# Moving six query transposes and their copy behind the last value product of batch 0, in a one-core attention and feed-forward kernel

## The chip, the cores and the metric

The kernel runs on one core of a Trainium2 chip. The core has five engines with queues of their own: TensorE (PE in the profile, PEld for its weight loads), VectorE (DVE), ScalarE (ACT), GpSimd (POOL) and SyncE (SP, which here only issues DMAs). The metric is the device time of one execution in microseconds (us); less is better.

## The reference

Attention over 4 batches and 8 heads of 768 positions with head size 64. Heads 0, 2 and 6 are causal over all positions ("retrieval"); the five others see four sink positions and a window of 64. The outputs of the eight heads stand side by side as 512 features of 3072 tokens and go through a two-layer network with a PReLU between the layers.

```python
mask = np.where(retr[0, :, 0, 0, None, None], full_mask, stream_mask)
scores = np.where(mask[None, :, :, :], scores, -1000000000.0)
a = np.exp(scores - np.max(scores, axis=-1, keepdims=True))
a = a / (np.sum(a, axis=-1, keepdims=True) + 1e-09)
attn_out = np.matmul(a, v)
x = attn_out.transpose(0, 2, 1, 3).reshape(B * S, H * D)
h = x @ w_in                                  # 512 -> 2048
g = np.maximum(h, 0.0) + alpha * np.minimum(h, 0.0)
out = g @ w_out                               # 2048 -> 512
```

## The kernel before, in words

Everything is a named item, and the list `ORDER` at the head of the file says in which order the items are put into the program (the loop at line 809). There is no scheduler behind it: each engine runs its own instructions in the order in which `ORDER` names them, and waits by semaphores for what it needs from the others. So moving a name in the list moves its instructions in the queue of each engine on which it has any, and nowhere else.

Attention works on pairs of heads. Number n = 4 * batch + pair, with the pairs (2,6), (1,5), (0,4), (3,7). So n = 3 is the last pair of batch 0 (heads 3 and 7, both windowed), and n = 5 is the second pair of batch 1 (heads 1 and 5). The items that matter here, with the engine that runs them:

- `Lq5`, `Cq5`: load of the queries of n = 5 (SP) and their cast to bf16 (`cast_q`, line 317; POOL for n = 5 and n = 4).
- `Tq5`: `to_array`, line 365, six 128x128 transposes on TensorE of the cast queries into one PSUM bank. `tq5`: `put_q`, line 370, one copy of that bank by ScalarE into the transposed queries qT. `Tk4` and `tk4.0`, `Tq4` and `tq4` are the same for other keys and queries.
- `S3.1.0`, `S3.1.1`: scores of n = 3, second head (TensorE, matmuls of line 415, each with a mask matmul of line 503). `s3.1.0`, `s3.1.1`: their exponentials (ScalarE, line 525). `S3.1.0` fills two banks and is the last score item of batch 0.
- `A3.0`, `A3.1`: the value product of each head of n = 3, 13 matmuls with the exponentials as weights (`AV`, line 554). `a3.0`, `a3.1`: division by the row sums (VectorE, lines 564 and 565).
- `X3`, `x3`: seven transposes of the result of n = 3 (TensorE, line 579) and the copy into xT (VectorE, line 584).
- `P0.2.0` and the like: matmuls of the first layer (`P1`, line 599) for token block 0 and feature block 2. In the first blocks they are split by head pair, part 0 being the pairs n = 0 and 1 (two matmuls), part 1 n = 2 (one), part 2 n = 3 (one). `p...` (line 604, ScalarE) and `g...` (line 611, VectorE) do the PReLU and free the bank. `O...` (line 619) is the second layer.

The batches overlap: the head of batch 1 (loads, casts, transposes) lies between the end of the attention of batch 0 and its feed-forward work. PSUM has eight banks. `take` gives an item the bank among its choices that was freed longest ago in the order of the list, and `give` records the freeing; so which bank an item gets is fixed by the order alone, when the program is built.

The part of the order around the change, before it:

```
... s3.1.1 S3.1.0 x1 P0.0.0 x2 P0.0.1 A3.0 P0.1.0 P0.1.1 Tq5 tq5 Lk6 Lq4 Lq6 Ck4.1 kfz3 nr
Cv3.1 s3.1.0 A3.1 Lv7 Lv5 Lq7 Ck5.0 wi3 a3.0 P0.2.0 P0.3.0 P0.3.1 a3.1 X3 x3 ns kfz1 P0.2.1
Tk4 near2 P1.2 ...
```

Of the kernel before, what the change touches and what calls it, by code (L numbers as in the profile page):

```python
# [25 lines left out]
g0.11 m8.0.2 tk5.1 wo2 Lv6 Lv4 P0.10 P0.8 p0.8 Tk7 g1.10 wo3 Cq4 Lk9 P0.12 P1.8 p0.10 g0.8 p0.12 g0.10 Tq4 P0.6 P0.9
p0.3 Ck6.1 g0.3 tq4 P0.4.0 P0.5.0 Tk6 P0.4.1 p1.8 g1.8 tk7.0 p0.9 g0.9 Cq6 P0.5.1 P0.5.2 p0.5 g0.12 p0.6 tk6.1 P0.4.2
g0.6 g0.5 tk6.0 S4.0.5 P0.7 p0.7 P1.6 g0.7 P1.4 s4.0.5 p0.4 Tq6 m4.1.2 tk7.1 g0.4 Cv5 p1.6 g1.6 O0.1.0 tq6 S4.0.3
O0.2.0 O0.2.1 S5.1.1 S5.0.0 S4.0.1 S6.1.0 m14.0.2 p1.4 g1.4 s5.0.0 O0.1.1 s4.0.3 s4.0.1 O0.2.2 S5.0.2 S5.1.0 S4.0.2
S5.1.2 s6.1.0 m4.0.1 Cv7 O0.3.0 s5.0.2 s5.1.2 s5.1.1 s4.0.2 O0.1.2 s5.1.0 O0.1.3 o0.1 Cq7 Cv4 O0.3.1 m5.1.0 m8.1.2  # L30
m5.0.2 m4.0.3 m5.1.2 S4.0.0 S4.1.4 S5.0.1 S4.0.4 S4.1.0 s4.0.4 s5.0.1 Lk10 m5.0.1 O0.2.3 O0.3.2 Tq7 m5.0.0 o0.2 s4.1.0
m4.0.4 m5.1.1 A5.1 s4.0.0 m4.0.0 a5.1 O0.3.3 tq7 S7.0.0 S7.0.1 S4.1.3 S7.1.1 S6.0.5 S4.1.1 m4.0.5 s4.1.4 o0.3 Lq9
s4.1.3 Ck8 m4.1.3 A5.0 a5.0 X5 s4.1.1 A4.0 s7.0.0 s7.1.1 Lk11 Lq8 s7.0.1 a4.0 s6.0.5 near1 m7.0.0 m7.1.1 m4.1.0 O1.1.0
S7.1.0 S6.0.4 S7.0.2 S4.1.5 S6.0.1 S7.1.2 S6.1.1 O1.1.1 Cv6 s7.1.0 O1.0.0 s4.1.5 m7.0.1 s6.1.1 m4.1.5 m6.1.1 s7.1.2
m6.1.0 s7.0.2 m7.0.2 S6.0.2 S4.1.2 S6.1.2 S6.0.0 s6.0.4 s4.1.2 s6.0.1 s6.1.2 O1.0.1 m6.0.5 m7.1.0 m4.1.1 m4.1.4 m7.1.2
m6.1.2 S6.0.3 A4.1 s6.0.0 m6.0.0 m6.0.1 A7.1 O1.1.2 A6.1 s6.0.3 m6.0.4 m6.0.3 s6.0.2 a4.1 a6.1 A6.0 A7.0 a6.0 O1.1.3
O0.0.0 O0.0.1 O0.0.2 O1.0.2 m10.0.2 O1.0.3 O0.0.3 o0.0 X4 X6 a7.1 a7.0 X7 P2.9 P2.3 p2.9 P3.4 Ck9 Cq9 g2.9 P2.14 p2.14
g2.14 Cq8 p3.4 Lq10 Lq11 Dk8.0 P2.10 p2.10 Dk9.1 o1.0 p2.3 g2.3 g3.4 Dk8.1 P3.2 P3.14 P3.12 P2.8 Dq8 P2.1 P3.8 o1.1
p3.2 Dk9.0 Lv10 g2.10 Dq9 p3.14 P2.7 Ck10 g3.2 p3.12 g3.12 g3.14 P2.2 p2.2 g2.2 Cq10 Dq10 P2.11 p2.1 g2.1 p2.11 p2.8
g2.11 P3.6 P2.5 p2.5 g2.5 P2.13 p2.13 g2.8 g2.13 P2.0 p2.0 g2.0 p2.7 P3.0 p3.0 P2.4 S8.0.5 Lv8 Lv11 P2.15 P2.12 s8.0.5  # L40
Cq11 g3.0 p2.15 g2.7 g2.15 S8.0.0 p2.12 g2.12 Ck11 p3.6 S9.0.2 P2.6 p2.6 g3.6 s8.0.0 p2.4 g2.4 g2.6 s9.0.2 p3.8 P3.10
g3.8 p3.10 O3.0.0 O2.0.0 S8.1.5 s8.1.5 O3.0.1 O2.0.1 g3.10 m8.0.0 Cv8 S8.1.3 S9.0.0 S8.0.3 S9.1.1 S8.0.1 S9.1.0 s8.1.3
s9.1.0 s8.0.1 s9.0.0 s8.0.3 m8.0.3 m8.0.1 O2.0.2 O2.0.3 o2.0 Dk10.1 Lv9 m9.0.0 Cv9 m8.0.5 Dk11.0 m9.1.0 m9.0.2 S8.0.4
S9.0.1 S10.1.1 S8.1.4 Dq11 s8.1.4 Lq13 Lk13 O3.0.2 Dk10.0 s9.1.1 s10.1.1 s9.0.1 s8.0.4 O3.0.3 o3.0 Dk11.1 S10.1.0
S10.1.2 m9.0.1 S11.0.2 S9.1.2 S8.0.2 S11.0.0 s9.1.2 Cv10 m9.1.1 A9.0 s11.0.2 s10.1.0 O2.3.0 m9.1.2 A9.1 a9.0 a9.1 X9
s10.1.2 s11.0.0 O2.3.1 Lq15 Lv14 Lq12 S8.1.0 S11.0.1 S10.0.3 m10.1.0 s8.0.2 S10.0.1 S8.1.2 S8.1.1 S10.0.0 O2.3.2
s8.1.2 s8.1.0 m8.1.4 Cq13 s11.0.1 s8.1.1 m11.0.2 m10.1.2 m8.0.4 m11.0.0 A8.0 s10.0.0 m8.1.5 m10.1.1 O2.3.3 a8.0
S11.1.2 S10.0.4 S11.1.0 S10.0.5 S10.0.2 m8.1.3 m11.0.1 s10.0.3 s10.0.1 S11.1.1 s11.1.2 A10.1 s11.1.1 O2.2.0 O2.1.0
s10.0.4 m6.0.2 m10.0.1 Cv11 m8.1.1 m8.1.0 a10.1 m10.0.4 Ck13 m10.0.0 m11.1.2 A11.0 A8.1 O2.1.1 s10.0.2 s10.0.5 o2.3
s11.1.0 Dk13.0 m11.1.1 m10.0.3 m10.0.5 m11.1.0 A10.0 a11.0 a8.1 a10.0 O3.1.0 A11.1 Cq12 O2.2.1 O2.2.2 O2.2.3 a11.1 X8  # L50
O2.1.2 O3.1.1 O3.1.2 X10 o2.2 O3.1.3 O2.1.3 X11 P4.11 o2.1 P4.14 P5.14 p5.14 P4.4 P4.6 Lk12 P5.0 g5.14 Ck12 p4.4 p4.6
p4.11 P4.13 g4.6 p4.14 g4.11 Lq14 g4.14 P5.12 P4.5 P4.12 p4.13 Dq12 o3.1 p5.0 g4.13 Cq14 g5.0 Dk13.1 p4.5 g4.5 g4.4
Cv14 P4.9 p4.9 g4.9 P4.2 P5.2 Dq13 p5.12 g5.12 P4.10 p5.2 P4.8 P4.1 p4.12 g4.12 g5.2 p4.10 g4.10 Lv15 Dk12.0 Dk12.1
Lv12 p4.1 Lk14 Lv13 Lk15 g4.1 P4.7 P4.0 p4.2 g4.2 p4.8 g4.8 p4.0 p4.7 g4.7 P4.15 Cv12 S13.0.1 s13.0.1 S12.0.5 S12.0.3
P4.3 P5.4 g4.0 s12.0.3 p4.3 s12.0.5 S12.1.5 S12.0.1 S12.0.0 S13.1.1 s13.1.1 Dq14 g4.3 Cq15 Ck14 m12.0.3 O4.3.0 s12.1.5
s12.0.1 O4.3.1 O4.3.2 s12.0.0 p4.15 g4.15 P5.6 P5.10 S12.1.1 S12.0.4 S12.0.2 p5.4 S13.1.0 g5.4 p5.6 s12.0.4 Dk14.0
P5.8 s13.1.0 s12.0.2 p5.8 s12.1.1 m12.0.0 g5.6 O4.3.3 Ck15 p5.10 g5.8 m12.0.1 g5.10 m12.0.4 O5.1.0 Cv13 O5.1.1 O5.1.2
o4.3 Dk14.1 S14.1.1 S14.0.0 S12.1.4 S14.0.1 S14.1.0 S13.0.2 m12.1.1 s14.1.0 s13.0.2 O4.2.0 m12.0.5 A12.0 s14.0.1
s12.1.4 O5.1.3 Dk15.1 s14.1.1 Dk15.0 s14.0.0 a12.0 m14.0.1 Dq15 o5.1 O4.2.1 S13.1.2 S12.1.2 S14.1.2 S14.0.4 m13.1.0
m14.0.0 m13.0.1 S14.0.5 S13.0.0 O4.2.2 O4.2.3 s13.1.2 m13.1.2 m13.1.1 s13.0.0 s14.0.4 s14.0.5 m13.0.2 S12.1.0 m12.1.5  # L60
s14.1.2 S12.1.3 S15.0.0 S14.0.3 m13.0.0 A13.1 o4.2 s12.1.0 s12.1.2 A13.0 s15.0.0 O5.0.0 s12.1.3 s14.0.3 m14.0.4 Cv15
a13.1 O5.0.1 a13.0 S15.0.1 S15.0.2 m12.1.0 S15.1.0 S15.1.2 S15.1.1 S14.0.2 O4.1.0 s15.0.2 s15.1.0 m12.1.4 s14.0.2
s15.1.1 m14.1.1 m14.0.5 m14.1.2 m12.1.3 m14.1.0 A12.1 m14.0.3 A14.1 A14.0 a14.0 s15.1.2 a14.1 m15.0.2 s15.0.1 a12.1
O4.1.1 X13 O4.0.0 O4.0.1 O4.0.2 O4.0.3 m15.0.0 m15.1.1 O4.1.2 m15.0.1 m15.1.2 m15.1.0 A15.0 o4.0 A15.1 a15.0 O4.1.3
a15.1 O5.0.2 X15 O5.0.3 X14 x15 o4.1 o5.0 X12 P6.11 p6.11 P6.2 P6.15 P6.10 p6.10 P7.4 P6.0 P6.1 g6.11 g6.10 p6.1 P6.6
P7.8 p6.15 g6.15 g6.1 p6.0 g6.0 P6.5 p7.4 p6.5 p6.6 g7.4 g6.6 g6.5 P6.3 P6.12 P7.2 p6.3 p6.12 g6.12 p6.2 g6.2 P6.4
p7.8 P7.6 P6.14 g6.3 g7.8 p7.6 p6.4 g7.6 g6.4 P7.10 P6.7 P6.8 p6.8 p6.7 P7.0 P6.9 P6.13 g6.7 p7.2 g7.2 g6.8 p7.10
g7.10 p6.9 P7.14 O6.3.0 P7.12 p6.13 g6.13 p7.12 O6.0.0 O6.0.1 O6.1.0 p7.0 g7.0 g6.9 O6.3.1 O7.0.0 O6.3.2 O6.1.1 p7.14
p6.14 g6.14 g7.12 O6.3.3 o6.3 O6.0.2 O6.1.2 O6.1.3 o6.1 O6.0.3 o6.0 O6.2.0 O6.2.1 O6.2.2 O7.0.1 O7.0.2 O6.2.3 o6.2
m12.0.2 g7.14 L2 l2 O7.0.3 o7.0 L0 L1 l1 warm1 l0  # L70
""".split()


# [776 lines left out]
```

## Time and profile before

| What | Value |
|---|---|
| Time, median of 3 runs | 231.12 us (231.07 to 232.63) |
| Time of the profiled execution | 231.47 us |
| Its span, first to last instruction | 229.8 us |
| Between the two, outside the span | 1.67 us |
| Mean granted TensorE clock | 1.000 |

Where the time goes by stretches of the span; PE, ACT and DVE are busy us:

| Stretch (us) | PE | ACT | DVE | DMA share | What runs |
|---|---|---|---|---|---|
| 27 to 29 | 2.00 | 0.00 | 1.19 | 1.22 | end of the attention of batch 0 |
| 29 to 31 | 0.40 | 1.51 | 0.26 | 1.18 | transposes of n = 5, their copy, exponential of n = 3 |
| 31 to 33 | 2.00 | 0.00 | 0.83 | 1.20 | last value product, first layer begins |
| 33 to 50 | 17.00 | 14.93 | 14.09 | 1.19 | first layer of batch 0, transposes of batch 1 |
| 50 to 57.2 | 6.89 | 6.81 | 4.59 | 1.10 | scores of batch 1 begin |
| 57.2 to 229.8 | 169.49 | 98.07 | 107.93 | 0.70 | the rest |

The trace gives, for each instruction, its start and duration on its engine, and for the idle time before it the engine or DMA whose signal ended it. A matmul's duration contains its way through the array, so that matmuls following one another overlap in the record: four of 512 columns take about 0.86 us, though each is shown with some 0.38. The DMA share is that of 16 DMA engines; values over 1 are overlapping packets.

### The profile page before, as it was taken

How to read it: one execution, taken by the hardware profiler on the slowest of the kernel's cores; microseconds unless marked ns; L12 is line 12 of the kernel's file. 1: busy time of each engine (PE TensorE's matmuls, PEld its weight loads, DVE VectorE, ACT ScalarE, POOL GpSimd, SP SyncE). 2: the span in 40 equal slices, each digit the busy share in tenths (PEclk: the TensorE clock that was granted, in tenths of full speed). 3: DMA queues.
4: the chain of work that ended last, by engine and by line, in shares of the span. 5: the costliest groups of instructions: out<-in, count | busy, mean ns of one | idle time of the engine just before them, and what ended most of it. 6: DMA issues, size and time to landing. Idle time of an engine off the chain costs nothing.

```text
span 229.8 us, 5247 instructions
## 1 busy us (share of the span) xinstructions
PE 221.8 (97%) x2005; PEld 135.1 (59%) x2005; DVE 148.9 (65%) x394; ACT 140.6 (61%) x285; POOL 45.9 (20%) x91
## 2 busy tenths in 40 slices
...
PEclk9999999999999999999999999999999999999999
...
GB/s 190 294 214 219 274 214 277 207 196 227 207 259 146 137 186 216 209 134 187 247 172 234 156 276 178 199 176 93 144 93 38 115 94 0 0 4 0 91 72 113
DMA packets 94957, 37.26 MB, mean 162 GB/s; under 512 B 81980, under 2 KB 93140, under 8 KB 94932
## 3 DMA queue, kind: packets, MB, share of 16 engines
...
q10 hardware_dynamic: 464, 0.40, 0.5%
q8 instruction: 15, 0.25, 0.4%
...
## 4 chain that ended last, share of the span: by engine, by line
PE 88%; ACT 3%; DMA 2%; issue 2%; SPq 1%; POOL 1%; DVE 0%; POOLq 0%; DVEq 0%; ACTq 0%
PE P L599 35%; PE P L619 34%; PE P L554 7%; PE P L432 4%; DMA kf<-in_k_dram 2%; PE P L365 2%; PE P L415 2%; PE P L638 2%; ACT neg L604 1%; PE P L503 1%; SPq L223 1%; PE P L579 1%; PE P L425 1%; ACT kT L394 1%; ACT eS L525 1%
## 5 line engine op out<-in xcount | busy, mean ns | idle before, releaser
L611 DVE SCALAR_TENSOR_TENSOR g<-neg,oma,P 128x256 bf16<-128x256 f32 (+1 forms) x128 | 71.1, 610 | 36.0 <-ACT neg L604 35.5
L599 PE MATMUL P<-xT,w_in_b 128*128 128x512 bf16 (+1 forms) x512 | 86.3, 326 | 0.0
L619 PE MATMUL P<-w_out_b,g 128*128 128x512 bf16 x368 | 85.4, 379 | 0.0
L604 ACT ACTIVATE neg<-P 128x512 f32<-128x512 f32 x96 | 54.1, 600 | 29.0 <-PE P L599 24.6
L599 PEld LDWEIGHTS <-w_in_b 128*128 128x128 bf16 x512 | 49.5, 98 | 31.9 <-DVE g L611 0.2
L619 PEld LDWEIGHTS <-g 128*128 128x128 bf16 x368 | 33.7, 98 | 37.3 <-issue 1.2
L471 ACT ACTIVATE eR<-P 128x448 bf16<-128x448 f32 (+4 forms) x63 | 37.2, 639 | 6.1 <-PE P L432 2.5
L625 ACT COPY ot<-P 128x512 f32<-128x512 f32 x23 | 13.9, 604 | 37.3 <-PE P L619 32.4
L629 POOL DMA_DIRECT2D out_dram<-ot x18 | 10.3, 571 | 115.0 <-ACT ot L625 114.8
L519 ACT ACTIVATE eS<-P 128x352 bf16<-128x352 f32 x45 | 21.0, 497 | 3.7 <-PE P L432 3.7
L565 DVE TENSOR_TENSOR xn<-P,rcp 128x448 bf16<-128x448 f32 (+1 forms) x32 | 19.5, 608 | 1.1
L530 DVE TENSOR_TENSOR eS<-eS,ms_near 128x352 bf16<-128x352 bf16 x45 | 14.5, 338 | 5.0 <-ACT eS L519 4.9
L481 DVE TENSOR_TENSOR eR<-eR,mr_near 128x128 bf16<-128x128 bf16 (+5 forms) x54 | 10.8, 228 | 4.4 <-ACT eR L471 4.4
L554 PE MATMUL P<-vb,eS 128*128 128x65 bf16 x260 | 10.8, 193 | 1.6 <-ACT eS L525 1.6
L564 DVE RECIPROCAL rcp<-P 128x7 f32<-128x7 f32 (+1 forms) x32 | 6.3, 198 | 9.2 <-PE P L554 9.0
L432 PE MATMUL P<-qT,kT 64*128 64x176 bf16 (+13 forms) x181 | 11.7, 251 | 0.3 <-DVE g L611 0.3
L554 PEld LDWEIGHTS <-eS 128*128 128x128 bf16 x260 | 9.5, 97 | 3.9 <-ACT eS L525 1.8
L432 PEld LDWEIGHTS <-kT 64*128 64x128 bf16 x181 | 7.2, 94 | 7.6 <-issue 6.4
L415 PE MATMUL P<-qT,kT 128*128 128x192 bf16 (+14 forms) x68 | 11.3, 251 | 0.3 <-ACT eS L525 0.3
L554 PE MATMUL P<-vb,eR 128*128 128x65 bf16 x276 | 10.1, 193 | 0.0
L554 PEld LDWEIGHTS <-eR 128*128 128x128 bf16 x276 | 9.4, 97 | 1.2
L647 DVE COPY ot<-P 128x128 f32<-128x128 f32 x1 | 0.3, 292 | 14.3 <-PE P L638 14.3
...
## 6 DMA issues: line engine op xcount, KB each, us to landing
...
```

The costliest lines, as they stand in the source:

```text
L415: nc.tensor.matmul(to, keys, queries, start=True, stop=stop)
L432: nc.tensor.matmul(to, keys[own], queries[own], start=True, stop=True)
L471: nc.scalar.activation(ebuf[n, hh][:, lo:hi].rearrange("p (x c) -> p x c", x=len(parts)), P[:, got[0]:got[0] + len(parts), 0:(hi - lo) // ...
L519: nc.scalar.activation(slots, sc[:, 0:352].rearrange("p (s c) -> p s c", c=176), AF.Exp, scale=scale)
L530: nc.vector.tensor_tensor(slots, slots, ms_near[:, 0:2, :] if m == 0 else ms_near[:, 1:3, :], op=ALU.mult)
L554: nc.tensor.matmul(pav[:, i, :], e[:, o:o + 128], vv[:, j, hh, 0:D + 1], start=(m == 0), stop=(m == len(terms) - 1))
L565: nc.vector.tensor_tensor(xn[n][:, 0:nt, D * hh:D * hh + D], pav[:, :, 0:D], rcp.to_broadcast([128, nt, D]), op=ALU.mult)
L599: nc.tensor.matmul(psg[:, w * i:w * (i + 1)], w_in_b[:, c, 128 * fb:128 * (fb + 1)], xT[:, c, o:o + w], start=(x == 0), stop=(x == 3))
L604: nc.scalar.activation(neg[t, f], bank(held["P", t, f][0]), AF.Relu, scale=-1.0)
L611: nc.vector.scalar_tensor_tensor(g_buf[t % 2][:, fb, 0:w], neg[t, f][:, c], oma[:, fb:fb + 1], bank(got[0])[:, c], op0=ALU.mult, op1=ALU.add)
L619: nc.tensor.matmul(bank(held["O", t, s][0]), g_buf[t % 2][:, f, 128 * s:128 * (s + 1)], w_out_b[:, f, :], start=(f == 0), stop=(f == 15))
L625: nc.scalar.copy(ot, bank(got[0]))
```

## The change

`Tq5` and `tq5` move down the list, from before `Lk6` to behind `P0.2.0`. Nothing else is moved.

```diff
-Ck4.0 s3.1.1 S3.1.0 x1 P0.0.0 x2 P0.0.1 A3.0 P0.1.0 P0.1.1 Tq5 tq5 Lk6 Lq4 Lq6 Ck4.1 kfz3 nr Cv3.1 s3.1.0 A3.1 Lv7 Lv5
-Lq7 Ck5.0 wi3 a3.0 P0.2.0 P0.3.0 P0.3.1 a3.1 X3 x3 ns kfz1 P0.2.1 Tk4 near2 P1.2 P0.1.2 P0.2.2 P0.0.2 p1.2 p0.1 g0.1
+Ck4.0 s3.1.1 S3.1.0 x1 P0.0.0 x2 P0.0.1 A3.0 P0.1.0 P0.1.1 Lk6 Lq4 Lq6 Ck4.1 kfz3 nr Cv3.1 s3.1.0 A3.1 Lv7 Lv5 Lq7
+Ck5.0 wi3 a3.0 P0.2.0 Tq5 tq5 P0.3.0 P0.3.1 a3.1 X3 x3 ns kfz1 P0.2.1 Tk4 near2 P1.2 P0.1.2 P0.2.2 P0.0.2 p1.2 p0.1
...
```

The remaining lines of the diff are the same list wrapped differently. On each engine this comes to:

- TensorE: the six transposes of `Tq5` now stand behind the 13 matmuls of `A3.1` and the two of `P0.2.0`, before the three of `P0.3.0` and `P0.3.1`.
- ScalarE: the copy `tq5` and the exponential `s3.1.0` change places.
- VectorE, POOL and SP: the same instructions in the same order.

The banks follow the order. `Tq5` gets bank 1 in place of 0, `P0.2.0` bank 0 in place of 1, `P0.3.0` bank 2 in place of 0 (freed by `s3.1.0`, no longer by `tq5`), `Tk4` bank 3 in place of 2, and `P1.2` bank 1 in place of 3 (freed by `tq5`, no longer by `s3.1.0`). From there on the four banks 0 to 3 are renamed among themselves to the end of the program, and each item's bank is freed by the same item as before. So the first matmul of `P1.2` has a new wait, for `tq5` on ScalarE.

More of the change, by code (lines that the diff above doesn't have):

```diff
@@ L21 @@
 A1.1 a2.0 tq3 s2.1.0 a1.1 S3.0.0 s2.1.1 s3.0.0 A2.1 a2.1 S3.1.1 X1 S3.0.1 s3.0.1 Lk5 wi4 kfz2 Cv3.0 Cq5 Lk7 wi2 X2
-Ck4.0 s3.1.1 S3.1.0 x1 P0.0.0 x2 P0.0.1 A3.0 P0.1.0 P0.1.1 Tq5 tq5 Lk6 Lq4 Lq6 Ck4.1 kfz3 nr Cv3.1 s3.1.0 A3.1 Lv7 Lv5
-Lq7 Ck5.0 wi3 a3.0 P0.2.0 P0.3.0 P0.3.1 a3.1 X3 x3 ns kfz1 P0.2.1 Tk4 near2 P1.2 P0.1.2 P0.2.2 P0.0.2 p1.2 p0.1 g0.1
-Ck5.1 P1.0 P0.3.2 g1.2 P0.15 tk4.0 p0.2 g0.2 p0.15 wo0 p1.0 Lk8 near0 g0.15 g1.0 ro1 P1.12 P1.14 m12.1.2 p0.0 g0.0 wo1
-tk4.1 p1.12 P0.14 g1.12 p0.14 g0.14 P0.13 p0.13 g0.13 P0.11 p1.14 Tk5 Ck7.1 g1.14 P1.10 tk5.0 p0.11 p1.10 Ck6.0 Ck7.0
@@ L26 @@
[L26 to L70, printed above, removed]
+Ck4.0 s3.1.1 S3.1.0 x1 P0.0.0 x2 P0.0.1 A3.0 P0.1.0 P0.1.1 Lk6 Lq4 Lq6 Ck4.1 kfz3 nr Cv3.1 s3.1.0 A3.1 Lv7 Lv5 Lq7
@@ new lines @@
+Ck5.0 wi3 a3.0 P0.2.0 Tq5 tq5 P0.3.0 P0.3.1 a3.1 X3 x3 ns kfz1 P0.2.1 Tk4 near2 P1.2 P0.1.2 P0.2.2 P0.0.2 p1.2 p0.1
+g0.1 Ck5.1 P1.0 P0.3.2 g1.2 P0.15 tk4.0 p0.2 g0.2 p0.15 wo0 p1.0 Lk8 near0 g0.15 g1.0 ro1 P1.12 P1.14 m12.1.2 p0.0
+g0.0 wo1 tk4.1 p1.12 P0.14 g1.12 p0.14 g0.14 P0.13 p0.13 g0.13 P0.11 p1.14 Tk5 Ck7.1 g1.14 P1.10 tk5.0 p0.11 p1.10
+Ck6.0 Ck7.0 g0.11 m8.0.2 tk5.1 wo2 Lv6 Lv4 P0.10 P0.8 p0.8 Tk7 g1.10 wo3 Cq4 Lk9 P0.12 P1.8 p0.10 g0.8 p0.12 g0.10 Tq4
+P0.6 P0.9 p0.3 Ck6.1 g0.3 tq4 P0.4.0 P0.5.0 Tk6 P0.4.1 p1.8 g1.8 tk7.0 p0.9 g0.9 Cq6 P0.5.1 P0.5.2 p0.5 g0.12 p0.6
@@ new lines @@
+tk6.1 P0.4.2 g0.6 g0.5 tk6.0 S4.0.5 P0.7 p0.7 P1.6 g0.7 P1.4 s4.0.5 p0.4 Tq6 m4.1.2 tk7.1 g0.4 Cv5 p1.6 g1.6 O0.1.0
+tq6 S4.0.3 O0.2.0 O0.2.1 S5.1.1 S5.0.0 S4.0.1 S6.1.0 m14.0.2 p1.4 g1.4 s5.0.0 O0.1.1 s4.0.3 s4.0.1 O0.2.2 S5.0.2
+S5.1.0 S4.0.2 S5.1.2 s6.1.0 m4.0.1 Cv7 O0.3.0 s5.0.2 s5.1.2 s5.1.1 s4.0.2 O0.1.2 s5.1.0 O0.1.3 o0.1 Cq7 Cv4 O0.3.1
+m5.1.0 m8.1.2 m5.0.2 m4.0.3 m5.1.2 S4.0.0 S4.1.4 S5.0.1 S4.0.4 S4.1.0 s4.0.4 s5.0.1 Lk10 m5.0.1 O0.2.3 O0.3.2 Tq7
+m5.0.0 o0.2 s4.1.0 m4.0.4 m5.1.1 A5.1 s4.0.0 m4.0.0 a5.1 O0.3.3 tq7 S7.0.0 S7.0.1 S4.1.3 S7.1.1 S6.0.5 S4.1.1 m4.0.5
@@ new lines @@
+s4.1.4 o0.3 Lq9 s4.1.3 Ck8 m4.1.3 A5.0 a5.0 X5 s4.1.1 A4.0 s7.0.0 s7.1.1 Lk11 Lq8 s7.0.1 a4.0 s6.0.5 near1 m7.0.0
+m7.1.1 m4.1.0 O1.1.0 S7.1.0 S6.0.4 S7.0.2 S4.1.5 S6.0.1 S7.1.2 S6.1.1 O1.1.1 Cv6 s7.1.0 O1.0.0 s4.1.5 m7.0.1 s6.1.1
+m4.1.5 m6.1.1 s7.1.2 m6.1.0 s7.0.2 m7.0.2 S6.0.2 S4.1.2 S6.1.2 S6.0.0 s6.0.4 s4.1.2 s6.0.1 s6.1.2 O1.0.1 m6.0.5 m7.1.0
+m4.1.1 m4.1.4 m7.1.2 m6.1.2 S6.0.3 A4.1 s6.0.0 m6.0.0 m6.0.1 A7.1 O1.1.2 A6.1 s6.0.3 m6.0.4 m6.0.3 s6.0.2 a4.1 a6.1
+A6.0 A7.0 a6.0 O1.1.3 O0.0.0 O0.0.1 O0.0.2 O1.0.2 m10.0.2 O1.0.3 O0.0.3 o0.0 X4 X6 a7.1 a7.0 X7 P2.9 P2.3 p2.9 P3.4
@@ new lines @@
+Ck9 Cq9 g2.9 P2.14 p2.14 g2.14 Cq8 p3.4 Lq10 Lq11 Dk8.0 P2.10 p2.10 Dk9.1 o1.0 p2.3 g2.3 g3.4 Dk8.1 P3.2 P3.14 P3.12
+P2.8 Dq8 P2.1 P3.8 o1.1 p3.2 Dk9.0 Lv10 g2.10 Dq9 p3.14 P2.7 Ck10 g3.2 p3.12 g3.12 g3.14 P2.2 p2.2 g2.2 Cq10 Dq10
+P2.11 p2.1 g2.1 p2.11 p2.8 g2.11 P3.6 P2.5 p2.5 g2.5 P2.13 p2.13 g2.8 g2.13 P2.0 p2.0 g2.0 p2.7 P3.0 p3.0 P2.4 S8.0.5
+Lv8 Lv11 P2.15 P2.12 s8.0.5 Cq11 g3.0 p2.15 g2.7 g2.15 S8.0.0 p2.12 g2.12 Ck11 p3.6 S9.0.2 P2.6 p2.6 g3.6 s8.0.0 p2.4
+g2.4 g2.6 s9.0.2 p3.8 P3.10 g3.8 p3.10 O3.0.0 O2.0.0 S8.1.5 s8.1.5 O3.0.1 O2.0.1 g3.10 m8.0.0 Cv8 S8.1.3 S9.0.0 S8.0.3
@@ new lines @@
+S9.1.1 S8.0.1 S9.1.0 s8.1.3 s9.1.0 s8.0.1 s9.0.0 s8.0.3 m8.0.3 m8.0.1 O2.0.2 O2.0.3 o2.0 Dk10.1 Lv9 m9.0.0 Cv9 m8.0.5
+Dk11.0 m9.1.0 m9.0.2 S8.0.4 S9.0.1 S10.1.1 S8.1.4 Dq11 s8.1.4 Lq13 Lk13 O3.0.2 Dk10.0 s9.1.1 s10.1.1 s9.0.1 s8.0.4
+O3.0.3 o3.0 Dk11.1 S10.1.0 S10.1.2 m9.0.1 S11.0.2 S9.1.2 S8.0.2 S11.0.0 s9.1.2 Cv10 m9.1.1 A9.0 s11.0.2 s10.1.0 O2.3.0
+m9.1.2 A9.1 a9.0 a9.1 X9 s10.1.2 s11.0.0 O2.3.1 Lq15 Lv14 Lq12 S8.1.0 S11.0.1 S10.0.3 m10.1.0 s8.0.2 S10.0.1 S8.1.2
+S8.1.1 S10.0.0 O2.3.2 s8.1.2 s8.1.0 m8.1.4 Cq13 s11.0.1 s8.1.1 m11.0.2 m10.1.2 m8.0.4 m11.0.0 A8.0 s10.0.0 m8.1.5
@@ new lines @@
+m10.1.1 O2.3.3 a8.0 S11.1.2 S10.0.4 S11.1.0 S10.0.5 S10.0.2 m8.1.3 m11.0.1 s10.0.3 s10.0.1 S11.1.1 s11.1.2 A10.1
+s11.1.1 O2.2.0 O2.1.0 s10.0.4 m6.0.2 m10.0.1 Cv11 m8.1.1 m8.1.0 a10.1 m10.0.4 Ck13 m10.0.0 m11.1.2 A11.0 A8.1 O2.1.1
+s10.0.2 s10.0.5 o2.3 s11.1.0 Dk13.0 m11.1.1 m10.0.3 m10.0.5 m11.1.0 A10.0 a11.0 a8.1 a10.0 O3.1.0 A11.1 Cq12 O2.2.1
+O2.2.2 O2.2.3 a11.1 X8 O2.1.2 O3.1.1 O3.1.2 X10 o2.2 O3.1.3 O2.1.3 X11 P4.11 o2.1 P4.14 P5.14 p5.14 P4.4 P4.6 Lk12
+P5.0 g5.14 Ck12 p4.4 p4.6 p4.11 P4.13 g4.6 p4.14 g4.11 Lq14 g4.14 P5.12 P4.5 P4.12 p4.13 Dq12 o3.1 p5.0 g4.13 Cq14
@@ new lines @@
+g5.0 Dk13.1 p4.5 g4.5 g4.4 Cv14 P4.9 p4.9 g4.9 P4.2 P5.2 Dq13 p5.12 g5.12 P4.10 p5.2 P4.8 P4.1 p4.12 g4.12 g5.2 p4.10
+g4.10 Lv15 Dk12.0 Dk12.1 Lv12 p4.1 Lk14 Lv13 Lk15 g4.1 P4.7 P4.0 p4.2 g4.2 p4.8 g4.8 p4.0 p4.7 g4.7 P4.15 Cv12 S13.0.1
+s13.0.1 S12.0.5 S12.0.3 P4.3 P5.4 g4.0 s12.0.3 p4.3 s12.0.5 S12.1.5 S12.0.1 S12.0.0 S13.1.1 s13.1.1 Dq14 g4.3 Cq15
+Ck14 m12.0.3 O4.3.0 s12.1.5 s12.0.1 O4.3.1 O4.3.2 s12.0.0 p4.15 g4.15 P5.6 P5.10 S12.1.1 S12.0.4 S12.0.2 p5.4 S13.1.0
+g5.4 p5.6 s12.0.4 Dk14.0 P5.8 s13.1.0 s12.0.2 p5.8 s12.1.1 m12.0.0 g5.6 O4.3.3 Ck15 p5.10 g5.8 m12.0.1 g5.10 m12.0.4
@@ new lines @@
+O5.1.0 Cv13 O5.1.1 O5.1.2 o4.3 Dk14.1 S14.1.1 S14.0.0 S12.1.4 S14.0.1 S14.1.0 S13.0.2 m12.1.1 s14.1.0 s13.0.2 O4.2.0
+m12.0.5 A12.0 s14.0.1 s12.1.4 O5.1.3 Dk15.1 s14.1.1 Dk15.0 s14.0.0 a12.0 m14.0.1 Dq15 o5.1 O4.2.1 S13.1.2 S12.1.2
+S14.1.2 S14.0.4 m13.1.0 m14.0.0 m13.0.1 S14.0.5 S13.0.0 O4.2.2 O4.2.3 s13.1.2 m13.1.2 m13.1.1 s13.0.0 s14.0.4 s14.0.5
+m13.0.2 S12.1.0 m12.1.5 s14.1.2 S12.1.3 S15.0.0 S14.0.3 m13.0.0 A13.1 o4.2 s12.1.0 s12.1.2 A13.0 s15.0.0 O5.0.0
+s12.1.3 s14.0.3 m14.0.4 Cv15 a13.1 O5.0.1 a13.0 S15.0.1 S15.0.2 m12.1.0 S15.1.0 S15.1.2 S15.1.1 S14.0.2 O4.1.0 s15.0.2
@@ new lines @@
+s15.1.0 m12.1.4 s14.0.2 s15.1.1 m14.1.1 m14.0.5 m14.1.2 m12.1.3 m14.1.0 A12.1 m14.0.3 A14.1 A14.0 a14.0 s15.1.2 a14.1
+m15.0.2 s15.0.1 a12.1 O4.1.1 X13 O4.0.0 O4.0.1 O4.0.2 O4.0.3 m15.0.0 m15.1.1 O4.1.2 m15.0.1 m15.1.2 m15.1.0 A15.0 o4.0
+A15.1 a15.0 O4.1.3 a15.1 O5.0.2 X15 O5.0.3 X14 x15 o4.1 o5.0 X12 P6.11 p6.11 P6.2 P6.15 P6.10 p6.10 P7.4 P6.0 P6.1
+g6.11 g6.10 p6.1 P6.6 P7.8 p6.15 g6.15 g6.1 p6.0 g6.0 P6.5 p7.4 p6.5 p6.6 g7.4 g6.6 g6.5 P6.3 P6.12 P7.2 p6.3 p6.12
+g6.12 p6.2 g6.2 P6.4 p7.8 P7.6 P6.14 g6.3 g7.8 p7.6 p6.4 g7.6 g6.4 P7.10 P6.7 P6.8 p6.8 p6.7 P7.0 P6.9 P6.13 g6.7 p7.2
```

3 lines of the change are left out of this document (added).

## The prediction

> **What bounds the kernel now.** I read the page first: how full is TensorE, and who carries the chain that ended last.
>
> ```profile
> PE 221.8 (97%) x2005; PEld 135.1 (59%) x2005; DVE 148.9 (65%) x394; ACT 140.6 (61%) x285; POOL 45.9 (20%) x91
> PEclk9999999999999999999999999999999999999999
> PE 88%; ACT 3%; DMA 2%; issue 2%; SPq 1%; POOL 1%; DVE 0%; POOLq 0%; DVEq 0%; ACTq 0%
> ```
>
> TensorE is busy 97% of the span and is 88% of the chain. A change that moves no work off it can only gain where TensorE stands still, so I looked for its gaps: the chain of waits in order of time, from 28 us on.
>
> ```profile
> 28.35 0.65 PE P L599 x3
> 29.00 0.35 PE P L365 x6
> 29.35 0.02 issue
> 29.37 0.80 ACT qT L370
> 30.17 0.72 ACT eS L525
> 30.89 0.05 issue
> 30.94 0.57 PE P L554 x13
> 31.51 1.08 PE P L599 x5
> ```
>
> The chain leaves TensorE for 1.6 us: `Tq5` (L365), then `tq5` on ScalarE (L370), then the exponential `s3.1.0` (L525), and only then `A3.1` (L554). The timelines of TensorE and of ScalarE say why; columns are start, duration, engine, line and, in brackets, the idle time before it and what ended it.
>
> ```profile
> 27.07 0.25 PE L503 MATMUL P<-nms,ident 128*128 128x192 bf16 x1
> 28.84 0.50 PE L365 MATMUL P<-ident,natq 128*128 128x128 bf16 x6
> 30.94 0.57 PE L554 MATMUL P<-vb,eS 128*128 128x65 bf16 x13 [1.60 <-ACT eS L525]
> 33.42 0.27 PE L599 MATMUL P<-xT,w_in_b 128*128 128x256 bf16 x1
> ```
>
> ```profile
> 29.37 0.80 ACT L370 COPY qT<-P 128x768 bf16<-128x768 bf16 x1 [2.55 <-PE P L365]
> 30.07 0.82 ACT L525 ACTIVATE eS<-P 128x768 bf16<-128x768 f32 x1
> 34.49 1.08 ACT L604 ACTIVATE neg<-P 128x512 f32<-128x512 f32 x2 [3.61 <-PE P L599]
> ```
>
> The last mask matmul of `S3.1.0` ends at 27.07 + 0.25 = 27.32. ScalarE was idle then, and idle until 29.37, because the copy that waits for `Tq5` stands ahead of the exponential in its queue. The exponential was ready 2.7 us before it ran.
>
> **The change part by part.** *ScalarE:* the exponential no longer stands behind the copy. It needs `S3.1.0` (27.32) and runs 0.82: done by about 28.2. *TensorE:* `A3.1` follows `P0.1.1`, whose slot ends where `Tq5` began, 28.84, so the exponential is 0.6 early. Its other inputs are there: the value cast of n = 3 and its sink copy end on VectorE at 27.65 (L308, 27.28 + 0.37), and its bank was freed by `x2`, which ends at 26.90 (L584). No matmul is added or removed, so I lay the same slots end to end. From starts in the timeline of before: 13 matmuls of `A3.1` take 31.35 - 30.94 = 0.41; one 512-column matmul 1.08 / 5 = 0.216; six transposes 0.34; `X3` 32.87 - 32.47 = 0.40; `P0.2.1` 0.21; `Tk4` 33.42 - 33.08 = 0.34.
>
> After: `A3.1` 28.84, `P0.2.0` 29.25, `Tq5` 29.68, `P0.3.0`/`P0.3.1` 30.02, `X3` 30.67, `P0.2.1` 31.07, `Tk4` 31.28, `P1.2` 31.62. Before, `P1.2` began at 33.42. Difference: **1.80 us**. (The bracket says 1.60 because six pipelined transposes end 0.16 after their slot; the rest is 0.04 that `X3` waited for `a3.1`.)
>
> What could stand in the way in this stretch:
> - `X3` needs `a3.1`. Before, the reciprocal began 0.60 after `A3.1` began and the division ended at 32.41, 1.47 after it: now 30.31, `X3` at 30.67. Covered, because `Tq5` lies between; without that cover it would cost the 0.04 of before.
> - `P1.2` has the new wait for `tq5`. The copy began 0.53 after `Tq5` began and takes 0.80: 29.68 + 1.33 = 31.01, and `P1.2` is due at 31.62. Nothing on ScalarE is between them: its next instruction is `p1.2`. Price zero, spare 0.6; behind it would wait the whole first layer, and the price would be the lateness itself.
> - The fourth matmul of `P1.2` needs `x3`; both shift together (33.63 against 33.74 before).
> - `tq5` is read by the scores of n = 5, after 57 us: being 0.85 later than before costs nothing.
> - POOL, SP and VectorE keep their lists. `Tk4`'s keys are cast on POOL by 28.48, and POOL does not wait for TensorE here.
>
> *After 31.62* everything on TensorE, ScalarE and VectorE is due 1.80 earlier. Only what does not move with them can take it back: transfers. `Tq4` is the first. This is POOL's cast for it, then its weight loads and the copy:
>
> ```profile
> 43.58 1.03 POOL L317 CAST natq<-qf 128x768 bf16<-128x768 f32 x1 [5.74 <-DMA qf<-in_q_dram]
> ...
> 46.13 0.43 PEld L365 LDWEIGHTS <-natq 128*128 128x128 bf16 x6
> ...
> 46.77 0.80 ACT L370 COPY qT<-P 128x768 bf16<-128x768 bf16 x1
> ...
> 50.39 0.60 ACT L604 ACTIVATE neg<-P 128x512 f32<-128x512 f32 x1 [0.31 <-ACT natq L317]
> ```
>
> POOL waited 5.74 for the queries of n = 4; the cast ends at 44.61. The weight load, due at 46.13 - 1.80 = 44.33, can start at about 44.65 (0.04 of handover, as from the exponential to `A3.1`). **0.32 is given back.** The chain runs through TensorE without a break from 33.58 to 50.09, so this loss stays: 1.80 - 0.32 = **1.48**. Bounds: 0 if the queries land 0.3 earlier, more by as much as they land later.
>
> The Trainium skill speaks against the full gain here ("DMA: Bandwidth & Descriptors", Latency and other measured facts): two of the sixteen DMA engines are usually slower, its guess being that software-generated descriptors crowd their ports. The trace has such traffic at that time, weight loads issued by POOL from 34.8 to 37.8 that took 10.6 to 18.3 us to land. By that rule the queries land when the slow engine is through, whatever TensorE does, and the gain is 1.48; if the load moved with TensorE it would be 1.80.
>
> Other loads, by the same test. `Cq6` runs on ScalarE at 49.24 without a visible wait; its load (384 KB) stands right behind that of n = 4 on SP, at 197 to 205 GB/s about 1.9 us, so I estimate it landed at 45.5; the bounds are 43.6 and 49.24, costing 0 to 1.48, and I take 0. `Cv4` on POOL ended a wait for values at 64.32, done at 65.25; `A4.0` used them at 68.47, so 1.7 is left. `Cv5`: 58.23 against 66.07. The weights of the first layer landed at most 11.3 after issue (30.84 for the last, so 42.2; needed at about 45). From 57 to the end TensorE is busy 169.5 of 172.6 us and the loads follow freed buffers, so the gain is carried to the end.
>
> Sum against the profiled execution: 231.47 - 1.48 = 229.99. The median of the runs was 0.35 below that execution, so 231.12 - 1.48 = **229.6**.
>
> **The rivals.**
> *A, the forecast:* the gap closes, `Tq4` gives some back: 1.2 to 1.8 saved, 229.3 to 229.9. Chance 0.76.
> *B, hidden by transfers or by ScalarE:* between 33 and 50 us ScalarE is busy 14.93 of 17.00 and the DMA share is 1.19; then the chain runs on ScalarE and VectorE from 50.39 to 57.19. If `Cq6` lands near 49.24, ScalarE waits there and all relu items queue behind it. For it: loads are late by any measure (5.74, later 12.69 for `Cv5`). Against: my estimate of 45.5, and that ScalarE's run of work itself starts 1.8 earlier (34.49 was a wait for TensorE). Saved 0 to 1.2: 229.9 to 231.1. Chance 0.13.
> *C, slower:* the queries of n = 4 land later than in this execution, and `Tq4` now blocks the first layer. Before, the spare was 1.5 (44.61 against 46.13); now it is gone, so each us of later landing is a us. It is slower than before from a landing 1.5 later, 45.1. Price: the slowest of the three runs was 1.5 over the median; if that became the rule, 1.5 more, 232.6. Against: SP's and POOL's issues are the same, so a late landing would have hurt before too. Chance 0.07.
> *D, more than the gap:* TensorE's 0.31 of idle time between 50 and 57.2 goes as well, and nothing is lost at `Tq4`: 2.1 saved, 229.0. Chance 0.04.
> That the change does not do what it says is hard to see: on ScalarE copy and exponential do change places, and the exponential had no other input.
>
> **How the numbers follow.** The likeliest is A: 229.6. For 8 in 10 the range runs from D's 229.0 to a little beyond B's end, 231.4, leaving out most of C. A measurement of this kernel tells about 1%, 2.3 us: below 228.8 or above 233.4. The visible gap is smaller than that, so A and B are all "same". Faster needs more than D, 0.04; slower needs C to be worse than its price, 0.06; same 0.90.
>
> **What would show it.** `A3.1` at about 28.9 with no wait for ScalarE; the exponential at 27.4; the copy at 30.2; `P1.2` at 31.6; `Cq4` still near 43.6 and the weight load of `Tq4` right behind its end, with idle time put down to POOL; a span near 228.3. I am wrong if `P1.2` waits for ScalarE, if `Cq6` shows a wait for its load, or if later items stand where they stood.

## The result, and the profile after

The changed kernel takes 229.64 us (median of 6 runs, 229.24 to 230.41), the kernel before on the same chip 231.09 us (6 runs, 230.35 to 232.63): ratio 0.994, with a 95% interval of 0.9912 to 0.9967, 1.45 us or 0.6% less. Its profiled execution took 230.41 us with a span of 228.7, and was the slowest of its six.

The page, same rows as before:

```profile
PE 222.8 (97%) x2005; PEld 136.3 (60%) x2005; DVE 150.2 (66%) x394; ACT 140.8 (62%) x285; POOL 45.8 (20%) x91
PEclk9999999999999999999999999999999999999999
PE 75%; DMA 12%; SPq 6%; ACT 3%; DVE 1%; issue 1%; POOL 0%; ACTq 0%; DVEq 0%
```

TensorE's clock and its share are as before. The chain has changed: 12% of it is now DMA. The chain of waits in order of time (start, duration, what) shows which:

```profile
26.32 17.29 DMA qf<-in_q_dram
43.61 0.05 issue
43.66 0.84 POOL natq L317
44.50 0.05 issue
44.55 0.51 PE P L365 x6
```

The chain is followed back from the end. It now arrives at `Tq4`, whose queries were the last thing to come, and so it leaves TensorE there and follows their load back to 26 us. The old gap, which lies beside that load, is no longer on it. That it is gone the timeline of TensorE shows:

```profile
28.61 0.56 PE L554 MATMUL P<-vb,eS 128*128 128x65 bf16 x13
29.00 0.59 PE L599 MATMUL P<-xT,w_in_b 128*128 128x512 bf16 x2
29.43 0.50 PE L365 MATMUL P<-ident,natq 128*128 128x128 bf16 x6
...
31.36 1.90 PE L599 MATMUL P<-xT,w_in_b 128*128 128x256 bf16 x13
```

`A3.1`, `P0.2.0`, `Tq5` and, after `P0.3`, `X3`, `P0.2.1` and `Tk4` (left out), `P1.2`: no bracket, so no wait. The reason stands in ScalarE's timeline:

```profile
27.12 0.81 ACT L525 ACTIVATE eS<-P 128x768 bf16<-128x768 f32 x1 [0.53 <-PE P L503]
29.97 0.80 ACT L370 COPY qT<-P 128x768 bf16<-128x768 bf16 x1 [2.04 <-PE P L365]
```

The exponential runs as soon as `S3.1.0` is done, and the copy after it.

**Where the gain went.** Two profiled executions do not begin alike (the table below has start-ups that differ by up to 1.15 us), so I subtract start times of the same TensorE instruction in the two traces and look at where the difference changes. At 27 us the profile of after is 0.23 ahead; from `P1.2` on 2.06 ahead, so the change has brought 1.83. Behind `Tq4` it is 1.68, behind `A5.1` (66 us) 1.06, and from there to the end it stays. So 0.38 and 0.62 are given back, at two places. (The brackets shown for them below, 0.21 and 0.45, are 0.17 smaller: they count from the end recorded for the matmul before, which lies behind its slot.) The first is the one forecast. This is TensorE:

```profile
44.55 0.51 PE L365 MATMUL P<-ident,natq 128*128 128x128 bf16 x6 [0.21 <-POOL natq L317]
```

The second is a surprise. Timeline of all engines in the profile of after:

```profile
63.36 0.59 DVE L530 TENSOR_TENSOR eS<-eS,ms_near 128x352 bf16<-128x352 bf16 x2 [1.81 <-ACT eS L519]
...
63.72 1.03 POOL L350 CAST vb<-vf 128x896 bf16<-128x896 f32 x1 [1.34 <-DMA vf<-in_v_dram]
...
63.87 0.95 DVE L481 TENSOR_TENSOR eR<-eR,mr_near 128x128 bf16<-128x128 bf16 x1
...
64.75 0.33 DVE L530 TENSOR_TENSOR eS<-eS,ms_near 128x352 bf16<-128x352 bf16 x1
...
65.13 0.45 PE L554 MATMUL P<-vb,eS 128*128 128x65 bf16 x9 [0.45 <-DVE eS L530]
```

And the same place in the profile of before:

```profile
64.32 0.93 POOL L350 CAST vb<-vf 128x896 bf16<-128x896 f32 x1 [0.27 <-DMA vf<-in_v_dram]
...
65.62 0.21 DVE L481 TENSOR_TENSOR eR<-eR,mr_near 128x128 bf16<-128x128 bf16 x1
```

A small mask multiply on VectorE (L481) took 0.95 us in place of 0.21. It began while POOL's cast `Cv4` (63.72 to 64.75) ran and ended at 64.82, 0.07 after it. Behind it in VectorE's queue stands the multiply (L530) whose weights `A5.1` loads, so TensorE stood 0.45. Before, the cast was over at 65.25 and the multiply began at 65.62. The multiply came 1.75 earlier, `Cv4`, which waits for a landing, only 0.6: so they now meet.

The Trainium skill ("SBUF — State Buffer", Who interferes with whom) has a rule for such a pair: a VectorE instruction with two inputs in SBUF contends with a GpSimd instruction that reads SBUF, because its second input comes through a port that the two engines share; the section calls this shared port pair an exclusive lock. The 0.95 against 0.21, and the end right behind POOL's, agree with it where POOL is first. They do not fit a multiply that does nothing at all until the cast has ended: alone it takes 0.21, and it ended 0.07 behind the cast. Whether it was already under way, or the end recorded for POOL is late, no run here shows.

### The profile page after: what moved, and what is told of

The parts are those of the page before. It is cut to its first block, busy times and chain, and to the rows that moved or that the text cites. A ratio compares the mean times of both kernels' runs of the same rounds, so it can differ in the third digit from the quotient of the medians.

```text
span 228.7 us, 5247 instructions
## 1 busy us (share of the span) xinstructions
PE 222.8 (97%) x2005; PEld 136.3 (60%) x2005; DVE 150.2 (66%) x394; ACT 140.8 (62%) x285; POOL 45.8 (20%) x91
## 4 chain that ended last, share of the span: by engine, by line
PE 75%; DMA 12%; SPq 6%; ACT 3%; DVE 1%; issue 1%; POOL 0%; ACTq 0%; DVEq 0%
PE P L619 33%; PE P L599 29%; DMA qf<-in_q_dram 8%; PE P L554 6%; PE P L432 4%; DMA vf<-in_v_dram 3%; SPq L246 2%; DMA kf<-in_k_dram 2%; PE P L638 2%; SPq L223 1%; SPq L248 1%; ACT neg L604 1%; SPq L209 1%; PE P L425 1%; ACT kT L394 1%
## 5 line engine op out<-in xcount | busy, mean ns | idle before, releaser
L530 DVE TENSOR_TENSOR eS<-eS,ms_near 128x352 bf16<-128x352 bf16 x45 | 14.4, 336 | 4.8 <-ACT eS L519 4.7
L481 DVE TENSOR_TENSOR eR<-eR,mr_near 128x128 bf16<-128x128 bf16 (+5 forms) x54 | 11.8, 246 | 4.0 <-ACT eR L471 4.0
```

The lines of the kernel that those rows point to most:

```text
L481: nc.vector.tensor_tensor(ej, ej, mask, op=ALU.mult)
L530: nc.vector.tensor_tensor(slots, slots, ms_near[:, 0:2, :] if m == 0 else ms_near[:, 1:3, :], op=ALU.mult)
```

## The experiments

The theory: the order of ScalarE's queue alone makes the gap, worth 1.8, and what is missing from it is given back where lateness that the gap used to hide comes through. The rivals: that the place of the transposes matters; that the landing of n = 4's queries always costs its 0.3; that the losses seen in one profile belong to the changed order, its renamed banks for instance, and not to what happens to run beside them; or that they are too rare to count.

In the table, "ahead" is the start of TensorE's instructions against the profile of before at 27 us (negative is earlier), and "kept" is what has been won from there to `P1.2`, to 57 us and to the end. All four are from the one profile of each run, by the subtraction above. "Span" is the median of the spans of all its executions.

| Run | ahead | kept: P1.2 | 57 us | end | median us (n) | ratio, 95% interval | span |
|---|---|---|---|---|---|---|---|
| after | -0.23 | 1.83 | 1.45 | 0.83 | 229.64 (6) | 0.994, 0.9912 to 0.9967 | 227.8 |
| after_again | -0.47 | 1.38 | 1.21 | 0.60 | 230.01 (12) | 0.9956, 0.993 to 0.9982 | 228.3 |
| after_third | -0.49 | 1.83 | 1.83 | 1.22 | 229.75 (12) | 0.9941, 0.9916 to 0.9965 | 227.8 |
| copy_only | 1.15 | 0.22 | 0.07 | 0.07 | 230.14 (12) | 0.9944, 0.9922 to 0.9966 | 228.05 |
| copy_again | -0.42 | 1.78 | 1.78 | 1.58 | 229.49 (1) | | |
| q4_first | -1.04 | 1.83 | 1.82 | 1.23 | 229.57 (6) | 0.9928, 0.9905 to 0.9952 | 227.85 |
| cv4_dve | -0.49 | 1.83 | 1.84 | 1.70 | 229.51 (6) | 0.9929, 0.9902 to 0.9957 | 227.75 |
| v3_act | -0.82 | 1.83 | 1.83 | 1.46 | 229.58 (7) | 0.993, 0.9906 to 0.9954 | 227.9 |
| v3_again | -0.64 | 1.84 | 1.84 | 1.84 | 229.71 (12) | 0.9926, 0.99 to 0.9952 | 227.95 |
| all_three | -0.39 | 1.84 | 1.84 | 1.71 | 229.41 (7) | 0.9929, 0.9904 to 0.9955 | 227.5 |
| all_again | -0.65 | 1.83 | 1.83 | 1.71 | 229.99 (12) | 0.9933, 0.9912 to 0.9954 | 227.75 |
| before_three | -1.03 | 0.00 | 0.00 | -0.13 | 231.23 (12) | 0.9999, 0.998 to 1.0018 | 229.45 |

The kernel before ran beside them on three chips: 231.27 (23 runs; with after_again, copy_only, q4_first, cv4_dve), 231.23 (19; with v3_act, all_three, before_three, copy_again) and 231.17 (29; with after_third, v3_again, all_again), spans 229.5, 229.4 and 229.4.

### The copy alone

`Tq5` stays; only `tq5` moves, in the kernel before.

```diff
-... P0.1.0 P0.1.1 Tq5 tq5 Lk6 Lq4 Lq6 Ck4.1 kfz3 nr Cv3.1 s3.1.0 A3.1 ...
+... P0.1.0 P0.1.1 Tq5 Lk6 Lq4 Lq6 Ck4.1 kfz3 nr Cv3.1 s3.1.0 tq5 A3.1 ...
```

> Half the change: only the copy tq5 goes behind the exponential s3.1.0 on ScalarE; the transposes Tq5 stay where they were on TensorE. Theory (the wait came from ScalarE's queue alone): the exponential starts at about 27.4, A3.1 directly behind Tq5, P1.2 at 31.6 as in the full change; time within 0.3 us of the changed kernel, 1.0 to 1.8 under the one before. Rival (the transposes ahead of A3.1 on TensorE are part of the cost): only part of it, half or less of the gain, since A3.1 still comes 0.34 later than in the full change and X3 then waits for a3.1.

230.14 us (12 runs, ratio 0.9944, 0.9922 to 0.9966), against 230.01 of the whole change on the same chip: as much, within what these runs can tell. Its profile is of the slowest of its executions, 232.55 us, and kept only 0.07. In it `A3.1` stood 1.31 us for VectorE, a wait that no other profile shows. VectorE, POOL and TensorE there:

```profile
29.25 2.55 DVE L308 COPY vb<-vb 4x192 f32<-4x192 f32 x1
...
30.34 1.27 POOL L661 TENSOR_SCALAR_AFFINE_SELECT mr_near<-one 128x1248 bf16<-128x1248 bf16 x1
...
31.86 0.49 PE L554 MATMUL P<-vb,eS 128*128 128x65 bf16 x11 [1.31 <-DVE vb L308]
```

The sink copy of `Cv3.1` (line 308) took 2.55 in place of the 0.37 of before, while POOL worked without a break from 29.29, and ended 0.19 behind the POOL instruction shown (31.61). This was seen once, and its cause is not shown. A second profile of the same kernel:

> The kernel with only the copy tq5 moved, a second profile of it. Theory: in an execution where Cv3.1 is not drawn out, A3.1 starts directly behind Tq5 and the distance from the start of Tq5 to that of P1.2 is 2.78 us (0.34 + 0.41 + 1.08 + 0.40 + 0.21 + 0.34), against 4.58 in the kernel before. Rival: 3.1 or more, because X3 waits for a3.1.

TensorE's timeline, then ScalarE's:

```profile
28.42 0.50 PE L365 MATMUL P<-ident,natq 128*128 128x128 bf16 x6
28.75 0.56 PE L554 MATMUL P<-vb,eS 128*128 128x65 bf16 x13
...
31.22 2.01 PE L599 MATMUL P<-xT,w_in_b 128*128 128x256 bf16 x14
```

```profile
26.93 0.81 ACT L525 ACTIVATE eS<-P 128x768 bf16<-128x768 f32 x1 [0.53 <-PE P L503]
28.95 0.80 ACT L370 COPY qT<-P 128x768 bf16<-128x768 bf16 x1 [1.21 <-PE P L365]
```

From `Tq5` to `P1.2` it is 31.22 - 28.42 = 2.80, against 33.42 - 28.84 = 4.58 before. The transposes stand where they stood, and 1.78 is won: what counts is that the copy no longer stands ahead of the exponential. The place of the transposes is worth the 0.05 that is left to the 1.83 of the whole change, about the 0.04 that the prediction named for `X3` waiting for `a3.1`.

### The changed kernel again

> The changed kernel once more, unchanged, for a second profile and more times. Theory (the gap at 29 us closes, and two things that keep the transfers' time take some back): 1.0 to 1.8 us under the kernel before, ratio 0.992 to 0.996; A3.1 follows P0.1.1 without a wait; the weight load of Tq4 starts right behind the end of the cast Cq4, wherever that lands; and the VectorE mask multiply near 64 us is long (0.9 us in place of 0.2) only if the POOL cast Cv4 runs at the same time. Rival (the second loss belongs to the changed order, for instance to the renamed banks): the same 0.6 us is lost at A5.1 in this profile too, at the same place, whenever Cv4 runs.

230.01 us, 1.26 under the kernel before. In its profile `Tk4` waited. TensorE, then POOL:

```profile
31.22 0.51 PE L365 MATMUL P<-ident,natm 128*128 128x128 bf16 x6 [0.27 <-POOL natm L330]
```

```profile
28.08 0.82 POOL L317 CAST natq<-qf 128x768 bf16<-128x768 f32 x1 [2.01 <-DMA qf<-in_q_dram]
...
30.66 0.51 POOL L330 CAST natm<-kf 128x384 bf16<-128x384 f32 x1 [0.68 <-DMA kf<-in_k_dram]
```

POOL waited 2.01 for the queries of n = 5 and then 0.68 for keys of n = 4. Both loads came late; the second wait is the one right before the cast that `Tk4` needs. 0.45 of the gain was lost. Another 0.17 went at 42.48, where the key transposes ahead of `Tq4` waited for a cast on VectorE (line 330). `Cq4` began at 43.09 and cost nothing: it ended at 43.91, and the weight load of `Tq4` began at 44.45, not right behind it as expected. L481 met `Cv4` again (0.98 us), now at `A5.0`: 0.61 lost. That is the same loss at another place, wherever the cast and the multiply meet, which speaks against the rival. A third profile,

> The changed kernel a third time, beside the two below on one chip, for the spread of its times. Theory (a late Cv3.1 takes the gain back in some executions): its times reach over 231 in one run of five or so, lowest 229.1, median 229.6 to 230.1. Rival (the spread is that of the loads in every kernel): its spread is that of the two below.

had `Cq4` at 39.99 and lost nothing at `Tq4`, but the collision was there: 0.61. Of its 12 times (median 229.75, 228.63 to 231.06) one was over 231. They spread as those of v3_again below (228.51 to 231.13), where `Cv3.1` is off VectorE, so a late `Cv3.1` is not what spreads them.

### The queries of n = 4 loaded first

`Lq4` is issued ahead of `Lk6`; the cast of the first half of these keys moves down the list for it.

```diff
-... P0.1.0 P0.1.1 Lk6 Lq4 Lq6 ...
+... P0.1.0 P0.1.1 Lq4 Lk6 Lq6 ...
-Ck6.0 Ck7.0 g0.11 ... p0.3 Ck6.1 g0.3 ...
+Ck7.0 g0.11 ... p0.3 Ck6.0 Ck6.1 g0.3 ...
```

> The changed kernel with the load of the queries of n = 4 put ahead of the load of the keys of n = 6 on SP, and the cast Ck6.0 moved down beside Ck6.1 so that VectorE does not wait for those keys. Theory (what is given back at Tq4 is the landing of these queries): the cast Cq4 runs 1 to 2.5 us earlier, the idle time of TensorE ahead of Tq4 (0.21 in the changed kernel) and of ScalarE ahead of tq4 (0.36) is gone, and the time is 0.2 to 0.4 under the changed kernel. Rival (the loss is made up later anyway, or the keys of n = 6 now come too late): no gain, or VectorE waits at Ck6.0 and the time is 0 to 1 over the changed kernel.

229.57 us, against 230.01 of the changed kernel on the same chip; the two intervals overlap, so the times do not tell them apart. The cast ran at 39.38 and nothing was lost at `Tq4`; the collision cost 0.6 at `A5.0`.

### `Cv4` on VectorE

Cast on VectorE behind `a5.1`, so that no cast of POOL runs beside the multiply.

```diff
-    CV = "PPPPPPVVVVVVVVVV"
+    CV = "PPPPVPVVVVVVVVVV"
-... o0.1 Cq7 Cv4 O0.3.1 ... A5.1 s4.0.0 m4.0.0 a5.1 O0.3.3 ...
+... o0.1 Cq7 O0.3.1 ... A5.1 s4.0.0 m4.0.0 a5.1 Cv4 O0.3.3 ...
```

> The changed kernel with the cast of the values of n = 4 on VectorE behind a5.1 in place of POOL. Theory (the mask multiply of VectorE is drawn out by the POOL cast that runs at the same time): no multiply of line 481 over 0.3 us between 60 and 68 us, A5.1 without a wait in its middle, and 0 to 0.6 us under the changed kernel, on average some 0.3, because the two do not meet in every execution. Rival (the multiply is long for another reason, its data or its bank): a multiply of 0.7 us or more near 64 us stays, and the time stays; or the cast of 0.62 us is too much for VectorE and A4.0 waits for it, 0 to 0.6 over.

229.51 us, against 230.01 of the changed kernel on the same chip, again with intervals that overlap. VectorE's timeline:

```profile
63.22 0.22 DVE L481 TENSOR_TENSOR eR<-eR,mr_near 128x128 bf16<-128x128 bf16 x1
...
65.17 0.62 DVE L350 CAST vb<-vf 128x896 bf16<-128x896 f32 x1
```

The multiply is back at 0.22, and the 0.6 is not lost. The cast takes 0.62 of VectorE, of which 0.14 is lost at about 70 us. So POOL's cast is what drew the multiply out. The other traces say so too: with the casts of n = 4 and n = 5 together they have ten multiplies of this size that began 0.02 to 0.54 after a 128x896 cast of POOL; they took between 0.47 and 0.99, the less the later they began, and every one ended 0.07 to 0.08 after the cast.

### `Cv3.1` on ScalarE

The value cast of `A3.1` and its sink copy leave VectorE.

```diff
-        cast_of("PV"[hh])(vv[:, :, hh, 0:D], vf[n % NF][:, :, hh, :])
-        sinks(n, ..., [hh], (nc.gpsimd.tensor_copy, nc.vector.tensor_copy)[hh])
+        cast_of("PA"[hh])(vv[:, :, hh, 0:D], vf[n % NF][:, :, hh, :])
+        sinks(n, ..., [hh], (nc.gpsimd.tensor_copy, nc.scalar.copy)[hh])
```

> The changed kernel with the value cast Cv3.1 and its sink copy on ScalarE in place of VectorE. Theory (with the wait on ScalarE gone, A3.1 waits next for Cv3.1, and that is drawn out by 1 us and more in some executions, when POOL's casts run beside it): the two ScalarE instructions take about 0.5 and 0.3 us ahead of the exponential s3.1.0, which then starts at most 0.3 later; A3.1 never waits for VectorE; the slowest times of the changed kernel (231.3 to 231.8) go, the median falls by 0.2 to 0.6, the lowest stays at 229.1. Rival (the spread of the changed kernel's times comes from elsewhere, the loads above all): the spread stays at 2.5 us and the median within 0.2.

229.58 us. L481 took 0.75 beside `Cv4`, and 0.37 was lost. Run again:

> The changed kernel with Cv3.1 and its sink copy on ScalarE, once more. Theory: no time over 230.5, median 0.2 to 0.5 under that of after_third. Rival: median within 0.2 of it and times over 231 as there.

229.71 us, highest 231.13: the spread did not go, and the median is that of the changed kernel on the same chip (229.75), as the rival has it. In this profile `Cv4` came 0.10 after the multiply had begun, and the multiply kept its 0.23. VectorE, then POOL:

```profile
64.09 0.23 DVE L481 TENSOR_TENSOR eR<-eR,mr_near 128x128 bf16<-128x128 bf16 x1 [0.56 <-ACT eR L471]
...
64.19 0.93 POOL L350 CAST vb<-vf 128x896 bf16<-128x896 f32 x1 [2.62 <-DMA vf<-in_v_dram]
```

`Cq4` came at 42.59, and all of the 1.84 was kept to the end, with `Cv4` on POOL and the banks of the changed kernel: so neither of them costs anything by itself.

### All three, with the change and without it

> The changed kernel with all three covers: queries of n = 4 loaded first and Ck6.0 lower, Cv4 on VectorE, Cv3.1 on ScalarE. Theory (the change saves 1.8 us, and three meetings with transfers and POOL casts give some of it back): 228.6 to 229.2, 1.8 to 2.5 under the kernel before, with a spread under 1 us; in the profile nothing is lost between 31 us and the end. Rival (the covers trade one wait for another): no faster than the better of its parts, 229.5.

> The kernel before with the same three covers (Cv3.1 ahead of tq5 on ScalarE, so that it does not stand behind the wait); against the run all_three this is the change alone. Theory: the wait of 1.6 to 1.8 us ahead of A3.1 is there, P1.2 starts 1.8 after that of all_three counted from the same start, and the time is 1.6 to 2.0 over all_three; against the kernel before it is within 0.6, since its wait hid a late Cv3.1 and its later Tq4 met the queries in time. Rival (the covers and not the change make the difference): it is within 0.5 of all_three.

(In the kernel without the change `Cv3.1` stands ahead of `tq5`, so that it does not queue behind it on ScalarE.)

229.41 us with the change, 231.23 without, on the same chip: the three edits alone bring nothing, and the change on top of them 1.8. TensorE of the kernel without it still has the gap:

```profile
27.81 0.50 PE L365 MATMUL P<-ident,natq 128*128 128x128 bf16 x6
29.91 0.57 PE L554 MATMUL P<-vb,eS 128*128 128x65 bf16 x13 [1.60 <-ACT eS L525]
```

Once more, beside a third run of the changed kernel:

> The changed kernel with all three covers, once more. Theory: 0.2 to 0.6 under after_third, lowest of the three, no time over 230.8. Rival: within 0.2 of v3_again and of after_third, so that the covers are worth less than these runs can tell.

229.99 us, against 229.75 of the changed kernel on that chip. What I expected of the three covers, less than 229.2 and a narrow spread, was wrong. The covers work in the traces, place by place; in the time they cannot be told from the change alone. Part of the reason is that what spreads the time is elsewhere: the highest run of all_three, 230.76, had a span of only 227.5, and 3.26 us outside the span, where 1.7 is usual. 20 of 176 executions had more than 2.3 there, 7 of 71 of the kernel before among them.

## Why the prediction was right

**The gap.** Right to 0.03. Forecast 1.80 between `P0.1.1` and `P1.2`; measured 1.83, and 1.78 to 1.84 in nine of the eleven profiles with the copy behind the exponential. The other two are after_again, 1.38 (`Tk4`), and copy_only, 0.22 (the sink copy). Slots laid end to end held: `A3.1` to `P1.2` was forecast as 31.62 - 28.84 = 2.78, and is 31.36 - 28.61 = 2.75. The new wait of `P1.2` for `tq5` cost nothing, as forecast: the copy is done at 30.77.

**`Tq4`.** Right in after's own profile (forecast 0.32, measured 0.38), but wrong as a fixed term. I took the landing at 43.6 as given. The same load was cast at 39.99, 43.09 and 43.66 in three executions of the same kernel, and `Tq4` lost nothing in the first two. The Trainium skill's page that I held against the full gain ("DMA: Bandwidth & Descriptors", Latency and other measured facts) speaks of two usually slower DMA engines; no run here separates the engines, so whether they set this landing stays open.

**`Cv4`: the step that failed.** The prediction asked when `A4.0` needs these values, found 1.7 to spare and priced it at nothing. That was the wrong question: the cast's consumer had time, but the cast itself held up a multiply on VectorE, and VectorE's work had moved by more than the landing. It cost 0.61 to 0.62 in the three profiles of the changed kernel, 0.6 in q4_first, 0.37 in v3_act and about 0.2 in copy_again; and nothing where the cast was on VectorE, began after the multiply (v3_again) or ended before it (copy_only).

**`Tk4` and `Cv3.1`.** Both were priced at nothing from one profile, in which they had time. One of the three profiles of the changed kernel shows `Tk4` late, by 0.45; none of the others in the table does. In after's profile the cast of `Cv3.1` on VectorE took 0.89, in place of 0.42, and its sink copy still ended 0.8 before `A3.1`; that it can cost something was seen in copy_only's profile alone, and how often it does stays open.

**The sum.** 1.48 forecast, 1.45 measured by the medians; 1.26 and 1.42 in the repeats. The agreement is partly luck: in after's profile it is 1.83 - 0.38 - 0.62 = 0.83, and 0.23 of an earlier start. The profiles of the changed kernel, all three from executions above their medians, kept 0.60 to 1.22; how often each loss happens in the others is not shown, since they have no trace. Their spans say that the losses vary: the middle half of 71 spans of before lies in 229.2 to 229.6, that of 30 of the changed kernel in 227.6 to 228.4. That fits a wait of 1.6 us having levelled out lateness that now comes through; no run isolates it.

**The rivals.** B: nothing was hidden by ScalarE or by `Cq6`; the difference of starts is constant from `Tq4` to 57 us. C: in no profile did the queries of n = 4 come more than 0.1 later than before; in most they came earlier. In all three sets of runs the changed kernel's median was below that of the kernel before. D: 2.1 was not reached; 1.84 is the most that any profile kept.
